# Three classical blocks and three pairs of whole blocks in pass 1, with attention packed into fewer steps

## Chip, cores and metric

The kernel runs on one core of one Trainium2 chip. The metric is the device time of one launch in microseconds. An execution taken with the profiler has a time of its own, which stands beside the median of the unprofiled runs.

## What is computed

The reference is a softmax linear attention followed by two mixture-of-experts layers with one expert each. All data are float32.

```python
q_s = softmax(q, axis=-1)             # q, k, v: (8, 8, 576, 64)
k_s = softmax(k, axis=2)              # over the 576 positions
kv  = einsum('bhsd,bhse->bhde', k_s, v)
x   = einsum('bhsd,bhde->bhse', q_s, kv)
x   = x reshaped to (4608, 512)       # tokens x model width
h   = x @ w_in;  g = h * sigmoid(1.702 h);  x = g @ w_out      # moe, w_in 512x2048
h   = x @ w_in;  g = where(h >= 1, h, where(h <= -1, 0, (h + 1)**2 / 4));  out = g @ w_out   # moe2
```

## The kernel before

Every factor of a large product is split into a high and a low part in the fast matmul type, and each product is three matmuls: high by high, high by low, low by high. A "step" of the classical form is 512 tokens (a block, of which there are nine) by 128 columns of w_in: four slices of the model width by three, so 12 matmuls of 512 columns (`gemm1`, L1038 to L1040, into `hps`). A step of the other form (`gemm_b`, L1360, into `z` and `zx`) is one of seven products of Strassen's scheme over a pair of halves: also 12 matmuls, of as many columns as a half has tokens. Seven such steps do the work of eight classical steps of that many columns; there are four groups of seven, `g`, in a pair.

The program has four passes, one for each weight. Pass 1 multiplies by the first w_in. Its first 64 steps are the classical blocks `CL`, 0, 1, 2 and 4. Between them, attention for all nine blocks is computed: SP loads k, v and q; VectorE takes maxima of k (`m`, `mx`), TensorE transposes them (`pa`, L884) and spreads them (`pb`), VectorE subtracts (`kt`, L900), ScalarE takes the exponentials, TensorE makes `pk` (k by v), VectorE divides it to `kv`; on the q side VectorE makes `qm`, `qt`, `qz` and the division `qt<-qt,qz`, TensorE transposes (`pt`, L981) and multiplies by `kv` (`px`, L999). ScalarE and VectorE write a classical block's result to `x_sb` (`x_hi`, `x_lo`); any other block goes through `xs` to DRAM. Meanwhile VectorE and ScalarE make Strassen's sums of the first weight (`t_pieces`, eight times eleven VectorE operations and three ScalarE copies, in `ts` and `w`). After the 64 steps come the pairs `PAIRS`, with halves of 384, 448 and 448 columns, which read `xs` back; in that stage w_out of the first layer is loaded raw and converted (`Weights("out1")`, conversion at L178 on ScalarE) and its products are stored for pass 2. Pass 2 starts at L1517; passes 3 and 4 are L605 and L487.

Nothing of pass 1's order is written by hand. `Plan` collects pieces: an engine, an estimated length `ns`, a rank in steps, names read and written, and for transfers `moves`, the time that the memory is busy. `order` simulates the engines by these estimates, takes at each moment the piece that can start first (the lowest rank among those that can start then), and so fixes each engine's order. `LATE` is the delay that it puts between a piece and its readers. Ranks are in units of a step of TensorE: attention of block j starts at `AT[j]`, and a new block starts every 6 steps.

Of the kernel before, what the change touches and what calls it, by code (L numbers as in the profile page):

```python
# [17 lines left out]
class Plan:  # L18
# [14 lines left out]
    def add(self, engine, ns, rank, fn, reads=(), writes=(), moves=0, take=0, give=0, haste=0, table=None):  # L33
        self.pieces.append(
            (rank, len(self.pieces), engine, ns, fn, reads, writes, moves, take, give, rank - haste, table)
        )

    def order(self):
        pieces = sorted(self.pieces, key=lambda x: x[:2])
        wrote, read, needs, after = {}, {}, [], [[] for _ in pieces]  # L40
        for n, (_, _, _, _, _, reads, writes, *_) in enumerate(pieces):
            deps = {wrote[r] for r in reads if r in wrote}
            for w in writes:
                deps |= {wrote[w]} if w in wrote else set()
                deps |= set(read.pop(w, ()))
                wrote[w] = n
            for r in reads:
                read.setdefault(r, []).append(n)
            deps.discard(n)
            needs.append(len(deps))  # L50
            for d in deps:
                after[d].append(n)
        since = [0] * len(pieces)
        free = dict.fromkeys(self.LATE, 0)
        open_to = {e: [n for n, x in enumerate(pieces) if x[2] == e and not needs[n]] for e in free}
        banks, moved, out, table = [0] * self.banks, 0, [], None

        def when(e, n):
            take = pieces[n][8]
            if take > len(banks):  # L60
                return None
            return max(free[e], since[n], sorted(banks)[take - 1] if take else 0)

        while len(out) < len(pieces):
            best = None
            for e, ns in open_to.items():
                starts = [(t, n) for n in ns if (t := when(e, n)) is not None]
                if starts:
                    first = min(t for t, _ in starts)
                    pick = min((pieces[n][10], n) for t, n in starts if t <= first)[1]  # L70
                    if best is None or first < best[0]:
                        best = first, e, pick
            start, e, n = best
            _, _, _, ns, _, _, _, moves, take, give, _, needed = pieces[n]
# [24 lines left out]
def kernel(  # L99
# [18 lines left out]
    CL = (0, 1, 2, 4)  # L118
# [4 lines left out]
    NB = NT // TB  # L123
# [88 lines left out]
    class Weights:  # L212
# [16 lines left out]
        def load(self, si, i, put):  # L229
# [14 lines left out]
            put(0, "SP", 560, fn, (), self.raw_n[i], moves=10.5 * n)  # L244
# [141 lines left out]
    O_AT = {"s7": 20, "u2": 21, "c11": 22, "c12": 23, "u3": 20, "c22": 23, "d11": 23}  # L386
# [201 lines left out]
    def pass_in(xq, sl, hooks):  # L588
# [140 lines left out]
        def later(k0, lag=1):  # L729
            def put(k, engine, ns, fn, reads, writes, moves=0):  # L730
                add(engine, ns, k0 + k, fn, reads + step(int(k0 + k) - lag), writes, moves, haste=H[5])
            return put
# [62 lines left out]
    AT = {0: (-20, -14), 1: (1, 5)}  # L795
    AT.update({j: (8.6 + 6.0 * (j - 2), 8.6 + 3.3 + 6.0 * (j - 2)) for j in range(2, NB)})
# [219 lines left out]
    def x_hi(j, c):  # L1016
        if c == 0:
            x0 = (20, 8)[j % 2]
# [34 lines left out]
    def keys(b, first, n, u):  # L1053
# [4 lines left out]
        def put(k, engine, ns, fn, reads, writes, **kw):  # L1058
            add(engine, ns, u + k, fn, reads, writes, **kw)
# [21 lines left out]
    def attention(j, at):  # L1081
        b = j if j < B else None
        x = CL.index(j) % 2 if j in CL else 0
        if b is not None:
            n = 1 if j == 0 else 2
            for first in range(0, 2, n):
                keys(j, first, n, at[first] + (4 if j else 0))
        for p in range(2):
# [5 lines left out]
            def put(k, engine, ns, fn, reads, writes, u=u, **kw):  # L1094
                add(engine, ns, u + k, fn, reads, writes, **kw)

            v0 = at[0] + (3.1 + 1.4 * p if j > 1 else 1.6 + 3 * p + V_AT) if j else u + V_AT
            if b is not None:
                k0 = (at[0] - 1 + 2 * p if j > 1 else at[0] - 6 + 4.3 * p) if j else u - 6
                put(k0 - u, "SP", 1120, lambda p=p: load_k(b, p), step(int(k0) - 1),  # L1100
                    tuple(nk[0] + (i,) for i in range(2)), moves=1800)
            put(-5, "SP", 1120 * (2 if j else 1), lambda t=t: load_q(t), step(int(u) - 6), nf, moves=1600)
            if b is not None:
                for h in range(5):
                    by = 0.25 if j > 1 else V_BY
                    put(v0 - u + h * by, "SP", 600, lambda p=p, h=h: load_v(b, p, h),
# [19 lines left out]
            at_px = 10 + (at[1] - u) * (j == NB - 1) + p / 10  # L1126
# [34 lines left out]
    add("PE", 0, AT[NB - 1][1] + 10.86, new_slots, px + old_t, sl(*BUSY))  # L1161
    add("PE", 0, AT[NB - 1][1] + 10.85, new_banks, px + old_t, (("bank", 2), ("bank", 3)))
# [51 lines left out]
    def t_pieces(u, m):  # L1214
        g, ns = m // 2, 90 + 1.06 * 256
        rows, k = (m, m + 1), [u]
# [5 lines left out]

        def part(x):
            return t_raw[x] if isinstance(x, int) else f32(t_at(x[0], *rows)[x[1]])

        def name(x):
            return (("ts", x),) if isinstance(x, int) else w_names(x[0], g)[x[1]:x[1] + 1]
# [4 lines left out]
        def high(p, x):  # L1232
            do("ACT", lambda: copy(t_at(p, *rows)[0], t_raw[x]), (("ts", x),) + free, w_names(p, g)[:1])

        def low(p, x):
            do("DVE", lambda: tt(t_at(p, *rows)[1], t_raw[x], part((p, 0)), ALU.subtract),
                (("ts", x),) + w_names(p, g)[:1] + free, w_names(p, g)[1:])
# [77 lines left out]
    PAIRS = ((384, 0), (448, 768), (448, 1664))  # L1315
# [3 lines left out]
    EB = ((24, 25, 26, 18, 19) * 7)[:32] + (E1 + E2) * 2  # L1319
# [113 lines left out]
    def later(k0, lag=1, haste=-3):  # L1433
        def put(k, engine, ns, fn, reads, writes, moves=0):
            add(engine, ns, k0 + k, fn, reads + step(int(k0 + k) - lag), writes, moves, haste=haste)
# [4 lines left out]
    hand(AT[NB - 1][1] + 10.88, sl(*WB), w_new.names)  # L1440
    NEXT = LAST + len(steps)
    w_new.everything([AT[NB - 1][1] + 11 + 5.3 * i for i in range(8)], lambda k: later(k, 1, 1))
# [260 lines left out]
```

## Time and profile before

| | us |
|---|---|
| median of 3 runs | 1516.66 |
| lowest and highest | 1516.39 to 1518.07 |
| the profiled execution | 1521.21 |
| its span | 1519.2 |
| startup, to the first L1038 | 31.65 |
| classical stage, to the first L1360 | 234.59 |
| pairs, to the first L1517 | 202.41 |
| passes 2 to 4, to the end of the span | 1050.55 |

The granted TensorE clock is 0.995 of full speed over the span, which is the level of 2.4 GHz. TensorE is busy for 98% of the span. A row of the trace that ends in brackets gives the idle time before the instruction and what released it.

### The profile page before, as it was taken

The page shows a single profiled execution, that of the slowest core. Times are in us where ns is not written, and L with a number is a line of the kernel's source. Part 1 is how long each engine was busy: PE and PEld are TensorE (multiplying, and loading weights), DVE is VectorE, ACT ScalarE, POOL GpSimd, SP SyncE. Part 2 cuts the span into 40 slices and gives each one's busy share as a digit, 9 for nine tenths or more (in the row PEclk, how much of TensorE's full clock was granted, in tenths as well). Part 3 has the DMA queues.
Part 4 walks back from the last instruction along what each step waited for, and adds up shares of the span by engine and source line. Part 5 has one row for each costly group of instructions (what it writes and reads, how often), then busy time and mean ns, then how long its engine had stood idle before and what let it go on. Part 6 is the DMA issues. An engine that isn't in the chain of part 4 may idle for free.

```text
span 1519.2 us, 21451 instructions
## 1 busy us (share of the span) xinstructions
PE 1483.9 (98%) x7920; PEld 1298.7 (85%) x7920; DVE 1132.6 (75%) x1470; ACT 904.3 (60%) x1154; POOL 6.2 (0%) x27
## 2 busy tenths in 40 slices
PE   5999999999999999999999999999999999999998
PEld 3777777998998888879998788888999788888998
DVE  7999993664627798899885486767675878686885
ACT  5878884575744454555545587878777444343442
POOL 0000000000000000000000000000000000000000
PEclk9999999999999999999999999999999999999999
DMA  9977755878798866676859555555668971625341
GB/s 282 280 228 214 216 191 188 282 246 284 236 329 323 325 215 235 208 243 208 273 171 392 198 202 226 196 219 193 248 232 323 380 245 53 201 86 151 93 126 42
DMA packets 276457, 341.17 MB, mean 225 GB/s; under 512 B 97152, under 2 KB 235904, under 8 KB 274560
## 3 DMA queue, kind: packets, MB, share of 16 engines
q1 hardware_dynamic: 275552, 339.70, 66.3%
q8 instruction: 62, 1.02, 0.3%
q14 instruction: 43, 0.35, 0.1%
q10 hardware_dynamic: 800, 0.10, 0.0%
HBM read 196.08 MB, written 143.65 MB: 224 GB/s over the span
## 4 chain that ended last, share of the span: by engine, by line
PE 85%; DMA 8%; DVE 3%; issue 1%; SPq 1%; ACT 1%; DVEq 0%; ACTq 0%
PE z L1517 16%; PE z L605 12%; PE z L487 12%; PE zx L605 9%; PE zx L487 9%; PE z L1360 5%; PE hps L1038 4%; PE zx L1360 4%; PE hps L1040 4%; PE hps L1039 4%; PE zx L1517 3%; DVE s L209 2%; DMA g<-s 2%; DMA w<-in_moe_w_in_dram 1%; DMA wp_in<-s 1%
## 5 line engine op out<-in xcount | busy, mean ns | idle before, releaser
L209 DVE TENSOR_TENSOR s<-s,s 128x1024 fp32r<-128x1024 f32 (+7 forms) x692 | 607.5, 920 | 146.2 <-PE zx L487 32.0
L1517 PE MATMUL z<-s,w 128*128 128x512 f32 (+1 forms) x1440 | 297.2, 367 | 1.2 <-DVE s L209 1.2
L1517 PEld LDWEIGHTS z<-s,w 128*128 128x128 f32 x1440 | 262.0, 188 | 35.5 <-DVE s L209 1.9
L455 ACT ACTIVATE s<-s 128x1024 fp32r<-128x1024 f32 (+1 forms) x140 | 136.3, 976 | 175.2 <-PE zx L487 62.1
L1190 ACT ACTIVATE s<-s 128x1024 fp32r<-128x1024 f32 (+2 forms) x168 | 161.5, 968 | 117.9 <-PE z L1517 67.4
L487 PE MATMUL z<-s,w 128*128 128x512 f32 (+1 forms) x1008 | 210.6, 368 | 1.3 <-DVE s L209 1.3
L605 PE MATMUL z<-s,w 128*128 128x512 f32 (+1 forms) x960 | 206.9, 367 | 0.0
L487 PEld LDWEIGHTS z<-s,w 128*128 128x128 f32 x1008 | 183.7, 188 | 26.1 <-DVE s L209 1.8
L605 PEld LDWEIGHTS z<-s,w 128*128 128x128 f32 x960 | 175.1, 188 | 22.6
L605 PE MATMUL zx<-s,w 128*128 128x512 f32 (+1 forms) x720 | 160.3, 371 | 5.1 <-ACT s L1190 4.6
L605 PEld LDWEIGHTS zx<-s,w 128*128 128x128 f32 x720 | 132.8, 190 | 23.2 <-ACT s L1190 5.0
L487 PE MATMUL zx<-s,w 128*128 128x512 f32 (+1 forms) x648 | 135.1, 367 | 0.0
L487 PEld LDWEIGHTS zx<-s,w 128*128 128x128 f32 x648 | 117.9, 188 | 15.0
L1360 PE MATMUL z<-s,w 128*128 128x448 f32 (+1 forms) x576 | 117.1, 355 | 0.0
L1360 PEld LDWEIGHTS z<-s,w 128*128 128x128 f32 x576 | 105.6, 188 | 6.0
L1038 PE MATMUL hps<-s,w 128*128 128x512 f32 x256 | 104.7, 409 | 0.9 <-ACT s L1044 0.9
L1040 PE MATMUL hps<-s,w 128*128 128x512 f32 x256 | 100.5, 392 | 0.0
L1039 PE MATMUL hps<-s,w 128*128 128x512 f32 x256 | 100.3, 392 | 0.0
L1360 PE MATMUL zx<-s,w 128*128 128x448 f32 (+1 forms) x432 | 89.5, 356 | 3.9 <-ACT zx L1190 3.6
L1360 PEld LDWEIGHTS zx<-s,w 128*128 128x128 f32 x432 | 79.1, 188 | 9.4 <-ACT zx L1190 4.3
L282 ACT ACTIVATE s<-s 128x256 fp32r<-128x256 f32 x168 | 65.1, 409 | 30.0 <-DVE s L209 13.6
L209 DVE TENSOR_TENSOR s<-s,z 128x1024 f32<-128x1024 f32 (+2 forms) x58 | 63.7, 1099 | 23.7 <-PE z L605 8.0
(102 smaller groups left out, 1477.2 us busy)
## 6 DMA issues: line engine op xcount, KB each, us to landing
s<-g SPq DMA_DIRECT2D x96, 512.0 KB, 5.7
g<-s SPq DMA_DIRECT2D x80, 512.0 KB, 2.9
wp_out<-s SPq DMA_DIRECT2D x112, 256.0 KB, 2.7
w<-wp_out SPq DMA_DIRECT2D x14, 2048.0 KB, 13.5
g<-s SPq DMA_DIRECT2D x48, 384.0 KB, 3.3
s<-g SPq DMA_DIRECT2D x48, 384.0 KB, 4.3
s<-in_moe_w_out_dram SPq DMA_DIRECT2D x32, 512.0 KB, 5.0
wp_in<-s SPq DMA_DIRECT2D x56, 256.0 KB, 4.2
```

The source lines that it names most:

```text
L209: return nc.vector.tensor_tensor(out=o, in0=x, in1=y, op=op)
L282: nc.scalar.activation(out=hi, in_=src, func=ACTF.Copy, scale=-1.0 if neg else 1.0)
L455: first_of[s] = nc.scalar.activation(out=hi, in_=src, func=ACTF.Copy)
L487: nc.tensor.matmul(out=z[:, m, :n], lhsT=a, rhs=b[:, c, :], start=(at is not None and i == 0 and c == 0 and x == 0), stop=(i == 3 and c == ...
L605: nc.tensor.matmul(out=z[:, m, :n], lhsT=a, rhs=b[:, c, :], start=(p in OPENS and c == 0 and x == 0), stop=(c == 1 and x == 2), skip_group ...
L1038: nc.tensor.matmul(out=hps, lhsT=wh, rhs=ah, start=(kk == 0), stop=False)
L1039: nc.tensor.matmul(out=hps, lhsT=wh, rhs=al, start=False, stop=False)
L1040: nc.tensor.matmul(out=hps, lhsT=wl, rhs=ah, start=False, stop=(kk == KD - 1))
L1190: nc.scalar.activation(out=o, in_=x, func=ACTF.Copy)
L1360: nc.tensor.matmul(out=zb[jj, g, a][:, m, :n], lhsT=w[:, f], rhs=y[:, c, :], start=(p in OPENS and c == 0 and x == 0), stop=(c == 1 and x ...
L1517: nc.tensor.matmul(out=zs2[j, a][:, m, :n], lhsT=y, rhs=b[:, c, :], start=(first and c == 0 and x == 0), stop=(i == 3 and c == 1 and x == ...
```

## The change

Block 4 is no longer a classical block. There are 48 classical steps, for blocks 0, 1 and 2, and three pairs with halves of 512 columns, which are six whole blocks. Attention of a block now starts every 4 steps (`PACE`), with the ranks inside a block scaled by 4/6, so it ends at step 42.7 by its ranks and not at 58.8. The sums of the first weight start at steps 30, 40, 46 and 52 (20, 29, 38 and 47 before); the last two groups use a tile of another slot, `late`, and their ranks lie behind the classical stage. The first w_out's raw loads and conversions start at 42.8 and come every 5 steps. A raw weight load counts 2,500 ns more until its readers may start in the planner's simulation (`lands`). Several slots are dealt out anew. Passes 2 to 4 issue the same TensorE instructions in the same order.

```diff
-    CL = (0, 1, 2, 4)
+    CL = (0, 1, 2)
...
-            put(0, "SP", 560, fn, (), self.raw_n[i], moves=10.5 * n)
+            put(0, "SP", 560, fn, (), self.raw_n[i], moves=10.5 * n, lands=2500)
...
-            late = done + self.LATE[e]
+            late = done + self.LATE[e] + lands
...
-    AT = {0: (-20, -14), 1: (1, 5)}
-    AT.update({j: (8.6 + 6.0 * (j - 2), 8.6 + 3.3 + 6.0 * (j - 2)) for j in range(2, NB)})
+    PACE = 4.0
+    AT = {0: (-20, -14), 1: (0, 3)}
+    AT.update({j: (9 + PACE * (j - 2), 9 + 0.55 * PACE + PACE * (j - 2)) for j in range(2, NB)})
+    END = AT[NB - 1][1] + PACE / 0.6 + 0.85
...
-            add(engine, ns, u + k, fn, reads, writes, **kw)
+            add(engine, ns, u + k * f, fn, reads, writes, **kw)
...
+        f = PACE / 6 if j > 1 else 1
...
-    add("PE", 0, AT[NB - 1][1] + 10.86, new_slots, px + old_t, sl(*BUSY))
+    add("PE", 0, END, new_slots, px + old_t, sl(*BUSY))
...
-        rows, k = (m, m + 1), [u]
+        rows, k, ts = (m, m + 1), [u], ("ts", "tu")[g >= T_LATE]
...
+        def raw(x):
+            if ts == "ts":
+                return t_raw[x]
+            if "late" not in t_ops:
+                t_ops["late"] = slot(T_SLOT).rearrange("p a c -> p (a c)")
+            return t_ops["late"][:, 256 * x:256 * x + 256].rearrange("p (a f) -> p a f", a=1)
...
+    T_AT_STEP, T_LATE, T_SLOT = (30, 40, 46, 52), 2, 19
+    late = ("tu", 0), ("tu", 1)
+    hand(END + 0.03, sl(T_SLOT), late)
+    hand(T_AT_STEP[-1] + 1.9, late, sl(T_SLOT))
...
-            t_pieces((20, 29, 38, 47)[g] + m, 2 * g + m)
+            t_pieces(T_AT_STEP[g] + m, 2 * g + m)
...
-    PAIRS = ((384, 0), (448, 768), (448, 1664))
+    PAIRS = ((512, 0), (512, 1024), (512, 2048))
...
-    EB = ((24, 25, 26, 18, 19) * 7)[:32] + (E1 + E2) * 2
+    EB = ((24, 25, 26, 18) + (24, 25, 26, 18, 19) * 6)[:32] + (E1 + E2) * 2
...
-    w_new.everything([AT[NB - 1][1] + 11 + 5.3 * i for i in range(8)], lambda k: later(k, 1, 1))
+    w_new.everything([END + 0.14 + 5 * i for i in range(8)], lambda k: later(k, 1, 1))
...
-    hand(LAST - 15, even, sl(*QB.values()))
-    hand(LAST - 0.05, odd, sl(*CB[4], *CB[3]))
+    hand(LAST - 15, odd, sl(*QB.values()))
+    hand(LAST - 0.05, even, sl(*CB[4], *CB[3]))
...
-                operand_b(0, x, AT[NB - 1][1] + 10.9 + 0.9 * i if i < 5 else LAST + i - 3.8)
+                operand_b(0, x, END + 0.04 + 0.9 * i if i < 5 else LAST + i - 3.8)
```

VectorE, from the division that makes `kv` to the division of the queries, in the classical stage. `ts` and `w<-ts` are the sums of the first weight, `qz` and `qt` the queries, `mc<-pa` the keys' maxima of the next block. Before:

```order
L209 TENSOR_TENSOR kv_318<-pk,rs 128x256
L209 TENSOR_TENSOR w<-ts_326,w 128x256
L209 TENSOR_TENSOR w<-ts_327,w 128x256
L209 TENSOR_TENSOR ts_326<-w 128x256
L209 TENSOR_TENSOR ts_327<-w 128x256
L209 TENSOR_TENSOR qt<-qf,qm 128x4x4x64
L209 TENSOR_TENSOR ts_326<-ts_326,ts_327 128x256
L968 TENSOR_REDUCE qz<-qt 128x16
L209 TENSOR_TENSOR w<-ts_326,w 128x256
L972 TENSOR_SCALAR qz<-qz 128x16
L973 RECIPROCAL qz<-qz 128x16
L209 TENSOR_TENSOR qt<-qt,qz 128x1024
```

and now:

```order
L209 TENSOR_TENSOR kv_319<-pk,rs 128x256
L209 TENSOR_TENSOR qt<-qf,qm 128x4x4x64
L974 TENSOR_SCALAR qz<-qz 128x16
L975 RECIPROCAL qz<-qz 128x16
L209 TENSOR_TENSOR qt<-qt,qz 128x1024
L890 TENSOR_REDUCE mc<-pa 128x4
L944 TENSOR_REDUCE qm<-qf 128x16
L970 TENSOR_REDUCE qz<-qt 128x16
L209 TENSOR_TENSOR ts_328<-ts_328,ts_329 128x256
L974 TENSOR_SCALAR qz<-qz 128x16
L975 RECIPROCAL qz<-qz 128x16
```

Of the first kind six rows in twelve belonged to the weight's sums, of the second one in eleven; the queries of one half and the keys of the next block follow each other directly.

TensorE, around a transpose `pa` of the keys' maxima. Before, it stands alone between two steps:

```order
L1039 MATMUL hps<-s_971,w 128x512
L1040 MATMUL hps<-s_969,w 128x512
L1038 MATMUL hps<-s_969,w 128x512
L1039 MATMUL hps<-s_971,w 128x512
L1040 MATMUL hps<-s_969,w 128x512
L884 MATMUL pa<-ident,mx 128x128 x4
L1038 MATMUL hps<-s_1266,w 128x512
L1039 MATMUL hps<-s_1268,w 128x512
```

and now:

```order
L1042 MATMUL hps<-s_946,w 128x512
L918 MATMUL pk<-v_317,kt 64x65 x20
L918 MATMUL pk<-v_318,kt 64x65 x20
L983 MATMUL pt<-ident,qt 128x128 x8
L886 MATMUL pa<-ident,mx 128x128 x4
L1040 MATMUL hps<-s_945,w 128x512
L1041 MATMUL hps<-s_947,w 128x512
```

Now `pk` of both halves, the transposes of the queries (`pt`) and `pa` of the next block stand together with no step between them, so `pt` and `pa` have no large matmuls ahead of them that could cover a late VectorE.

ScalarE, in the stage of the pairs, around the conversion of a raw weight (L178, two halves) and the copy `zx<-z` that a step of TensorE needs. Before:

```order
L1395 ACTIVATE s_3072<-s_3072 128x2x384
L1190 ACTIVATE w<-even 128x256
L178 ACTIVATE s_2888<-s_2887 128x512
L1395 ACTIVATE s_3076<-s_3076 128x2x384
L1395 ACTIVATE s_3156<-zx 128x2x384
L178 ACTIVATE s_2888<-s_2890 128x512
L1190 ACTIVATE zx<-z 128x2x384
L1190 ACTIVATE w<-even 128x256
```

and now:

```order
L1409 ACTIVATE s_3272<-z 128x1024
L1193 ACTIVATE s_3274<-s_2803 128x1024
L1193 ACTIVATE s_3291<-s_2780 128x1024
L178 ACTIVATE s_2632<-s_2631 128x512
L1409 ACTIVATE s_3230<-s_3230 128x1024
L178 ACTIVATE s_2632<-s_2634 128x512
L1409 ACTIVATE s_3252<-s_3252 128x1024
L1193 ACTIVATE zx<-z 128x1024
```

The copy of the bank still stands behind both halves of the conversion, with one row between the second half and it, where before there was none.

## Rows read from the trace of the kernel before

**Rows 1.** The page: span, and TensorE's busy time, share and instructions

```profile
span 1519.2 us, 21451 instructions
PE 1483.9 (98%) x7920; PEld 1298.7 (85%) x7920; DVE 1132.6 (75%) x1470; ACT 904.3 (60%) x1154; POOL 6.2 (0%) x27
```

**Rows 2.** Waits of TensorE: line, releaser, us in total, times, longest

```profile
PE zx L1360 <- ACT zx L1190: 3.6, 2, 2.0
...
PE hps L1038 <- ACT s L1044: 0.9, 1, 0.9
```

**Rows 3.** Timeline of TensorE at three stage borders: start, length, line, shapes

```profile
31.65 0.78 PE L1038 MATMUL hps<-s,w 128*128 128x512 f32 x1
...
266.24 2.27 PE L1360 MATMUL z<-s,w 128*128 128x384 f32 x12
268.35 0.39 PE L1038 MATMUL hps<-s,w 128*128 128x512 f32 x1
...
468.65 1.54 PE L1517 MATMUL z<-s,w 128*128 128x512 f32 x6
```

**Rows 4.** The chain of waits: unbroken runs of matmuls, start, length, count

```profile
366.66 4.86 PE z L1360 x24
...
501.46 65.28 PE z L1517 x288
...
1052.07 4.18 PE z L605 x24
```

**Rows 5.** Windows: stretch, length, five engines' busy time, PEclk, DMA share, GB/s

```profile
37.00:227.10 190.10, 189.18 (x1530) 150.41 (x1529) 180.55 (x295) 159.44 (x186) 3.08 (x10) 1.00 0.79 226
60.00:80.00 20.00, 20.00 (x183) 15.22 (x182) 19.54 (x29) 18.86 (x21) 0.61 (x2) 1.00 1.04 269
180.00:200.00 20.00, 20.00 (x178) 16.12 (x176) 17.43 (x34) 15.42 (x20) 0.00 (x0) 1.00 0.84 257
266.20:468.60 202.40, 198.51 (x1021) 186.57 (x1021) 107.04 (x189) 118.72 (x178) 0.00 (x0) 1.00 0.81 280
```

**Rows 6.** VectorE's groups, 37 to 240 us: count, busy, mean ns, idle before

```profile
L900 DVE TENSOR_TENSOR kt<-kt,pb 128x1280 f32<-128x1280 f32 x14 | 20.5, 1483 | 0.5 <-PE pb L893 0.5
L209 DVE TENSOR_TENSOR qt<-qt,qz 128x1024 f32<-128x1024 f32 x16 | 19.6, 1225 | 0.6
...
L209 DVE TENSOR_TENSOR ts<-w 128x256 f32<-128x256 f32 x32 | 12.8, 419 | 0.1
...
L209 DVE TENSOR_TENSOR s<-px,s 128x512 fp32r<-128x512 f32 x14 | 9.2, 684 | 1.9 <-ACT s L1020 1.9
```

**Rows 7.** Timeline of VectorE, the last division of the queries in the classical stage

```profile
224.69 0.75 DVE L209 TENSOR_TENSOR ts<-w 128x256 f32<-128x256 f32 x2
225.36 0.17 DVE L972 TENSOR_SCALAR qz<-qz 128x16 f32<-128x16 f32 x1
...
225.85 1.23 DVE L209 TENSOR_TENSOR qt<-qt,qz 128x1024 f32<-128x1024 f32 x1
```

**Rows 8.** DMA issues, 30 to 240 us: count, KB each, median us to landing

```profile
g<-s SPq DMA_DIRECT2D x26, 512.0 KB, 4.3
v<-in_v_dram SPq DMA_DIRECT2D x55, 128.0 KB, 3.9
kt<-in_k_dram SPq DMA_DIRECT2D x12, 512.0 KB, 5.7
...
xs<-qT SPq DMA_DIRECT2D x8, 512.0 KB, 4.3
```

**Rows 9.** Who waited for the loads of k (line 848): us, times

```profile
  DVE m L209: 8.6, 5
```

**Rows 10.** Timeline of ScalarE and TensorE where a pair's step waited

```profile
285.04 0.69 ACT L178 ACTIVATE s<-s 128x512 f32<-128x512 f32 x1 [3.19 <-DMA s<-in_moe_w_out_dram]
...
288.48 0.68 ACT L178 ACTIVATE s<-s 128x512 f32<-128x512 f32 x1 [1.32 <-DMA s<-in_moe_w_out_dram]
...
289.91 2.35 PE L1360 MATMUL zx<-s,w 128*128 128x384 f32 x12 [1.97 <-ACT zx L1190]
```

More of the change, by code (lines that the diff above doesn't have):

```diff
@@ L31, in __init__, with add @@
         self.pieces, self.banks, self.chained = [], banks, chained
-    def add(self, engine, ns, rank, fn, reads=(), writes=(), moves=0, take=0, give=0, haste=0, table=None):
+    def add(self, engine, ns, rank, fn, reads=(), writes=(), moves=0, take=0, give=0, haste=0, table=None, lands=0):
         self.pieces.append(
-            (rank, len(self.pieces), engine, ns, fn, reads, writes, moves, take, give, rank - haste, table)
+            (rank, len(self.pieces), engine, ns, fn, reads, writes, moves, take, give, rank - haste, table, lands)
         )
@@ L73, in order @@
             start, e, n = best
-            _, _, _, ns, _, _, _, moves, take, give, _, needed = pieces[n]
+            _, _, _, ns, _, _, _, moves, take, give, _, needed, lands = pieces[n]
             ns += self.SWAP * (needed not in (None, table))
@@ L384, in bank @@
         return rooms["p", i].tile([P, 2, TB], FP32, tag=f"p{i}", name=name)
-    O_AT = {"s7": 20, "u2": 21, "c11": 22, "c12": 23, "u3": 20, "c22": 23, "d11": 23}
+    O_AT = {"s7": 20, "u2": 21, "u3": 23, "c22": 20, "d11": 20}
     T_AT = (22, 23)
@@ L729, in later, with put @@
         def later(k0, lag=1):
-            def put(k, engine, ns, fn, reads, writes, moves=0):
+            def put(k, engine, ns, fn, reads, writes, moves=0, lands=0):
                 add(engine, ns, k0 + k, fn, reads + step(int(k0 + k) - lag), writes, moves, haste=H[5])
@@ L1017, in x_hi @@
         if c == 0:
-            x0 = (20, 8)[j % 2]
+            x0 = (8, 20)[j % 2]
             x_sb[j] = [[slot(x0 + 2 * i + c, FP32R) for c in range(2)] for i in range(2)]
@@ L1051, in step, with keys @@
         return (("step", s),) if s >= 0 else ()
-    def keys(b, first, n, u):
+    def keys(b, first, n, u, f):
         ps = range(first, first + n)
@@ L1086, in attention @@
             for first in range(0, 2, n):
-                keys(j, first, n, at[first] + (4 if j else 0))
+                keys(j, first, n, at[first] + (4 * f if j else 0), f)
         for p in range(2):
@@ L1125, in attention @@
             need += tuple(("kv", bb, p) for bb in range(2))
[L1126 removed]
+            at_px = 10 + (at[1] - u) / f * (j == NB - 1) + p / 10
             put(at_px, "PE", 1000, lambda p=p: q4(j, p), need, (("px", p),), take=2)
@@ L1221, in do @@
             add(engine, ns, k[0], fn, reads, writes)
+        def raw(x):
[4 more added lines that the diff above has]
+            return t_ops["late"][:, 256 * x:256 * x + 256].rearrange("p (a f) -> p a f", a=1)
         def part(x):
-            return t_raw[x] if isinstance(x, int) else f32(t_at(x[0], *rows)[x[1]])
+            return raw(x) if isinstance(x, int) else f32(t_at(x[0], *rows)[x[1]])
         def name(x):
-            return (("ts", x),) if isinstance(x, int) else w_names(x[0], g)[x[1]:x[1] + 1]
+            return ((ts, x),) if isinstance(x, int) else w_names(x[0], g)[x[1]:x[1] + 1]
         def dve(o, x, y, op):
@@ L1232, in high @@
         def high(p, x):
-            do("ACT", lambda: copy(t_at(p, *rows)[0], t_raw[x]), (("ts", x),) + free, w_names(p, g)[:1])
+            do("ACT", lambda: copy(t_at(p, *rows)[0], raw(x)), ((ts, x),) + free, w_names(p, g)[:1])
         def low(p, x):
-            do("DVE", lambda: tt(t_at(p, *rows)[1], t_raw[x], part((p, 0)), ALU.subtract),
-                (("ts", x),) + w_names(p, g)[:1] + free, w_names(p, g)[1:])
+            do("DVE", lambda: tt(t_at(p, *rows)[1], raw(x), part((p, 0)), ALU.subtract),
+                ((ts, x),) + w_names(p, g)[:1] + free, w_names(p, g)[1:])
         def both(x, y, op):
@@ L1433, in later, with put @@
     def later(k0, lag=1, haste=-3):
-        def put(k, engine, ns, fn, reads, writes, moves=0):
-            add(engine, ns, k0 + k, fn, reads + step(int(k0 + k) - lag), writes, moves, haste=haste)
+        def put(k, engine, ns, fn, reads, writes, moves=0, lands=0):
+            add(engine, ns, k0 + k, fn, reads + step(int(k0 + k) - lag), writes, moves, haste=haste, lands=lands)
         return put
```

18 lines of the change are left out of this document (9 added, 9 removed).

## Prediction, made before the change was run

> **What bounds the kernel now.** I read the page first: TensorE is busy for 1483.9 us of a span of 1519.2, 98% [rows 1], so time can be saved only by giving TensorE less to do or by taking away the little idle time it has. Then its waits: in pass 1 it lost 3.6 us to a ScalarE copy in the pair stage and 0.9 us at `hps` [rows 2]. Then the borders of the stages: classical from 31.65, pairs from 266.24, pass 2 from 468.65, with one last classical step inside the pair stage, from 268.35 on [rows 3]. Last, the windows, for who is close behind TensorE: in the classical stage VectorE, busy for 180.55 of 190.10 us, with ScalarE at 159.44; in the pair stage nobody (VectorE 107.04, ScalarE 118.72 of 202.40) [rows 5]. So the change must be judged by two things: how many matmul columns go, and whether VectorE still keeps up when attention is packed more tightly.
>
> **Matmul columns.** Unbroken runs give the pace: 65.28 us for 288 matmuls of 512 columns, 226.7 ns each; 4.86 for 24 of 448, 202.5 ns; 4.18 for 24 of 384, 174.2 ns [rows 4]. Each step is 12 matmuls, each pair 28 steps, 336 matmuls. Before: 64 classical steps, 768 x 0.2267 = 174.1; pairs 336 x 0.1742 + 672 x 0.2025 = 194.6; 368.7 us. After: 48 classical steps, 576 matmuls, and 3 x 336 = 1008, all of 512 columns: 1584 x 0.2267 = 359.1. That is **-9.6**. All of it lies on the bottleneck, and nothing else runs on TensorE in its place: attention's small matmuls are the same in number.
>
> The Trainium skill ("TensorE: Matmul & The Clock Gate", section "Back-to-back issue gap") gives a fixed 2.5 ns on top of N/2.4 ns; this trace disagrees, with 226.7 where that makes 215.8. By the page the sum here would be -5.7 (an estimate), since wide matmuls would be worth less against narrow ones; the measured runs decide.
>
> **The pair stage.** It took 468.65 - 266.24 = 202.4 us, without the classical step (12 x 0.2267 = 2.7) 199.7, against 194.6 of pure matmul time. The excess is 5.1 us, and 3.9 of it can be named: 3.6 where `zx` waited for ScalarE [rows 2] and small change. The timeline shows how: ScalarE stood 3.19 us and then 1.32 us in front of a conversion whose raw weight had not landed, and the copy that TensorE's next step needed was queued behind it; TensorE lost 1.97 us [rows 10]. After, the planner puts 2.5 us between such a load and its conversion, so conversions should stand later in ScalarE's queue. But the copy still stands behind both halves of a conversion in the listing of after, so the mechanism isn't gone by construction; the real landing time decides. Steps are longer (2.72 us, not 2.1 to 2.4), which gives ScalarE more room for each. Bounds: 0 if no load is late, 5 if it goes as before. I take 2, nearer to the loads being in time, since only two of eight conversions cost TensorE anything before. Stage: **-5.1 + 2 = -3.1**. In this stage VectorE also gets the second half of the first weight's sums, some 44 operations of 0.34 to 0.42 us, 15 to 18 us; it had 95 us free there [rows 5], so that costs nothing as long as the sums come before the steps that read them, which the listing has some steps ahead.
>
> **The classical stage.** Its matmuls are counted above; what remains are waits. The stage before had 0.9 us of them at `hps` [rows 2], put there by a late result of attention; I count **-0.9** and then the new waits on their own. A new block came every 6 steps and now every 4. Per block TensorE has 4 x 2.72 = 10.9 us of steps and about 7.8 of attention: 234.6 us of stage less 63 x 2.72 = 171.4 is 63.2, over some eight blocks. So 18.7 us a block, where it was 24.1.
>
> VectorE has to fit in. I take the stretch from its second `kv` division to the last division of the queries, 37.0 to 227.1 in the trace: 190.1 us, VectorE busy for 180.55 of them [rows 5, 7]. In the listings the same stretch has 10 steps fewer on TensorE: 190.1 - 27.2 = 162.9 us. On VectorE it has 57 sums of the weight fewer (29 where there were 86) and 4 of the low-part subtractions `s<-px,s` fewer. A sum costs 12.8/32 = 0.40 by its group's busy time [rows 6], or 0.335 where two follow each other (224.69 to 225.36) [rows 7]; the subtraction 9.2/14 = 0.66 [rows 6]. So VectorE sheds 22 to 25.5 us and keeps 155 to 159 of work for 162.9 of TensorE's. If it never waits, it is in time on the average, and only its worst place is late. But before, it also stood idle for 9.6 us of the stretch, mostly behind others: 8.6 us in all for loads of k [rows 9], 1.9 for ScalarE [rows 6]. If it waits as much again, it needs 165 to 169 and TensorE loses 2 to 6. The listings say where: TensorE's `pt` waits for the division of the queries and `pa` for the maxima of k, and they now follow `pk` with no step between them, so a late VectorE is no longer covered by 2.72 us of matmuls. Behind a waiting `pt` everything on TensorE stands still, since its queue runs in order. ScalarE was busy for 159.44 of the stretch [rows 5]; if it shed nothing it would still fit into 162.9, and it sheds the copies that go with the 57 sums, so I count it at nothing.
>
> Memory is the other load. A block moves k and v, 1.18 MB each by their shapes, q and `xs` 1.05 each, and two stores of `g`, 0.52 each: 5.5 MB in 18.7 us, 294 GB/s, where the stretch has 226 now [rows 5, 8]. The nearest rows: at 60 to 80 us the engines were full (share 1.04) at 269 GB/s, so a block would take 5.5/0.259 = 21.3 us; at 180 to 200 they were at 0.84 with 257, so full would be 306 GB/s, 18.0 us [rows 5]. The two stand on either side of 18.7. I take new waits of **+6**: the upper end of VectorE's sum, with k's loads later than they were. Bounds: 0 (no waits) and 18.2 (memory at its slower rate, below).
>
> The Trainium skill ("DMA: Bandwidth & Descriptors", section "Specifications") gives about 358 GB/s as a core's share of the memory: 5.5 MB would take 15.4 us (an estimate) and not bind. It also asks for pieces of 512 bytes or more for full rate; the loads of v come in rows of 64 floats, 256 bytes, and the trace's 269 GB/s at full share bears that second rule out. It speaks against this change, and is the last rival below.
>
> **The rest.** Passes 2 to 4 have the same TensorE instructions in the same order. What may differ is how pass 2 is entered (its first operands and the conversions of the next weight); **-0.5**, with -1.5 to +2.
>
> **Sum.** -9.6 - 5.1 + 2 - 0.9 + 6 - 0.5 = -8.1. The profiled execution stands at 1521.21, so after it would be near 1513.1; the median 1516.66 is 4.55 lower than that execution, and the same difference on it gives **1508.6**.
>
> **Rivals.** (1) *Waits nearly vanish.* VectorE keeps 155 to 159 us of work for 162.9 and uses the difference; no new waits, pair stage at +1.5: -9.6 - 5.1 + 1.5 - 0.9 - 0.5 = -14.6, 1502.1. Against it: TensorE lost 0.9 us even at 24.1 us a block, and the cover between attention's groups is gone. (2) *The gain is eaten.* VectorE falls behind by its own waits at each of seven blocks, about 1.7 us each, W = 12 in place of 6: -2.1, 1514.6, no difference that can be told. For it: loads of k made VectorE wait 8.6 us already, and they are now asked for at a higher rate. Against it: VectorE has 4 to 8 us to spare over the stretch. (3) *Slower: memory becomes the bound of the blocks.* At the slower rate each of seven blocks takes 21.3 us and not 18.7, 18.2 in place of 6: +4.1, 1520.8. It decides from 14.1 us of waits on, that is 20.7 us a block. For it: share 1.04 at 60 to 80 us. Against it: at 180 to 200 nearly the same rate took a share of only 0.84. That the change doesn't do what it says (conversions as late as before) is worth 3 us and lies inside the range.
>
> **Chances.** Forecast 0.66, rival (1) 0.12, (2) 0.14, (3) 0.08. A measurement of this kernel tells apart about 0.2%, 3.0 us: faster is below 1513.6, slower above 1519.7. Forecast and (1) are faster, 0.78; (2) 0.14 the same; (3) 0.08 slower. The range: the forecast with its bounds (pair waits 0 to 5, classical waits 0 to 12, pass 2 -1.5 to +2, which will hardly all fall on one side), 1502.5 to 1515.0; it leaves out half of (1), some of (2) and all of (3), about 0.2.
>
> **What will show it.** In the trace of after: the first `gemm_b` near 31.65 + 234.6 - 15 x 2.72 + 5 = 230; the pair stage near 231 (228.5 of matmuls and 2 of waits); then passes 2 to 4 of the same length, 1050. Waits of TensorE at `pt`, `pa` or `hps` for VectorE of about 6 us; if they stand for DMA of k or v, (3) has begun. DMA share near 1 and VectorE with idle time in the blocks' windows would say memory; VectorE at 98 to 99% with TensorE waiting would say VectorE. Waits of `zx` for ScalarE should be below 3.6. The prediction is wrong if classical waits pass 11 us, or if the pair stage takes more than 234.

## The result, and the profile after

| | before | after |
|---|---|---|
| median of the runs, us | 1516.93 | 1502.25 |
| lowest and highest | 1516.39 to 1518.07 | 1501.48 to 1506.35 |
| the profiled execution / its span | 1521.21 / 1519.2 | 1501.64 / 1499.6 |
| startup, to the first step of gemm1 | 31.65 | 30.96 |
| classical stage | 234.59 | 195.16 |
| pairs | 202.41 | 228.48 |
| passes 2 to 4, to the end of the span | 1050.55 | 1045.0 |

The ratio of after to before is 0.9906, with a 95% interval from 0.9893 to 0.992: 14 us faster, between 12 and 16. Forecast were 1508.6, in a range from 1502.5 to 1515.0; the first rival, in which the waits nearly vanish, stood at 1502.1. So the median lies at the lower end of the range, a quarter of a microsecond outside it.

The span fell by 19.6 us and the median by 14.7. The execution that was profiled before stood 4.5 us above its median, so the stages of these two traces add up to more than the medians differ. One part of it recurs, though: pass 3 took 353.08 us before and 349.22 after, and in the other traces below it is likewise shorter wherever the change is in. What is behind that stands in the section on the prediction.

The page of after, its span and its busy row, as [rows 1]:

```profile
span 1499.6 us, 21008 instructions
...
PE 1470.7 (98%) x7728; PEld 1266.3 (84%) x7728; DVE 1140.2 (76%) x1466; ACT 899.2 (60%) x1138; POOL 6.2 (0%) x27
```

The timeline of TensorE at the borders of the stages, as [rows 3]. gemm1 now has the lines 1040 to 1042, a pair's step 1374, pass 2 1531:

```profile
30.96 0.76 PE L1040 MATMUL hps<-s,w 128*128 128x512 f32 x1
...
226.12 3.11 PE L1374 MATMUL z<-s,w 128*128 128x512 f32 x13
...
454.60 1.75 PE L1531 MATMUL z<-s,w 128*128 128x512 f32 x7
```

The pair stage is 454.60 - 226.12 = 228.48 us. Its 1008 matmuls at 226.7 ns are 228.5: not a gap is left in it. The chain of waits shows the pace, as [rows 4]:

```profile
226.28 5.44 PE z L1374 x24
231.72 2.72 PE zx L1374 x12
```

TensorE's waits after its start-up, over the whole span, as [rows 2]. No row of L1374 is left, and `hps` waits 1.4 us where it waited 0.9 (the rows of `pa` and `pb` mix in the start-up; what they wait in the classical stage stands below):

```profile
PE zx L605 <- ACT zx L675: 2.3, 1, 2.3
PE hps L1040 <- ACT s L1046: 1.4, 2, 0.8
PE z L487 <- DVE s L209: 1.2, 1, 1.2
```

Two windows of after, as [rows 5]: the stretch of blocks, and the pairs (columns: stretch, length, busy time of PE, PEld, DVE, ACT and POOL, granted clock, DMA share, GB/s).

```profile
37.00:200.00 163.00, 160.25 (x1404) 126.23 (x1403) 156.06 (x228) 133.39 (x152) 3.08 (x10) 1.00 0.89 261
...
226.20:454.60 228.40, 228.40 (x1010) 189.11 (x1008) 133.06 (x234) 138.05 (x193) 0.00 (x0) 1.00 0.74 270
```

The first window was given the length that the prediction worked out, 163 us, and in it VectorE has the work that was counted, 156.06 us (155 to 159), and 6.9 us of idle time where the prediction carried over 9.6. The stretch itself begins earlier than the prediction has it: the second division of `kv` starts at 31.75 in before, not at 37.0, and at 30.49 in after. From there to the end of the last division of the queries, before and after:

```profile
31.75:227.08 195.33, 194.41 (x1553) 153.81 (x1552) 185.59 (x302) 161.51 (x191) 3.08 (x10) 1.00 0.79 230
```

```profile
30.49:201.81 171.32, 168.57 (x1442) 132.28 (x1441) 164.03 (x241) 140.00 (x162) 3.08 (x10) 1.00 0.89 263
```

It became 24.0 us shorter, where 27.2 were counted. VectorE's idle time in it fell from 9.7 to 7.3 us, and TensorE's rose from 0.9 to 2.8.

### The profile page after: what moved, and what is told of

Same layout as the page of the kernel before. It is cut to its first block, busy times and chain, and to the rows that moved or that the text cites. A ratio compares the mean times of both kernels' runs of the same rounds, so it can differ in the third digit from the quotient of the medians.

```text
span 1499.6 us, 21008 instructions
## 1 busy us (share of the span) xinstructions
PE 1470.7 (98%) x7728; PEld 1266.3 (84%) x7728; DVE 1140.2 (76%) x1466; ACT 899.2 (60%) x1138; POOL 6.2 (0%) x27
## 4 chain that ended last, share of the span: by engine, by line
PE 89%; DMA 6%; DVE 3%; SPq 1%; issue 1%; ACT 1%; DVEq 0%; ACTq 0%
PE z L1531 20%; PE z L487 12%; PE z L605 12%; PE zx L605 9%; PE zx L487 9%; PE z L1374 9%; PE zx L1374 7%; PE zx L1531 3%; PE hps L1040 2%; PE hps L1042 2%; PE hps L1041 2%; DMA kt<-in_k_dram 1%; DMA qf<-in_q_dram 1%; DMA g<-s 1%; DMA s<-x 1%; PE px L1001 1%
## 5 line engine op out<-in xcount | busy, mean ns | idle before, releaser
L209 DVE TENSOR_TENSOR s<-s,s 128x1024 fp32r<-128x1024 f32 (+5 forms) x692 | 614.3, 927 | 157.7 <-ACT s L282 33.6
L1531 PE MATMUL z<-s,w 128*128 128x512 f32 (+1 forms) x1440 | 296.7, 367 | 0.0
L1531 PEld LDWEIGHTS z<-s,w 128*128 128x128 f32 x1440 | 262.1, 188 | 33.8
L455 ACT ACTIVATE s<-s 128x1024 fp32r<-128x1024 f32 (+1 forms) x140 | 136.2, 976 | 176.1 <-PE zx L487 62.1
L1193 ACT ACTIVATE s<-s 128x1024 fp32r<-128x1024 f32 (+1 forms) x168 | 164.9, 988 | 125.5 <-PE z L1531 87.6
L1374 PE MATMUL z<-s,w 128*128 128x512 f32 x576 | 136.4, 389 | 0.0
L1374 PEld LDWEIGHTS z<-s,w 128*128 128x128 f32 x576 | 108.1, 188 | 22.5
L1374 PE MATMUL zx<-s,w 128*128 128x512 f32 x432 | 103.8, 389 | 0.0
L1374 PEld LDWEIGHTS zx<-s,w 128*128 128x128 f32 x432 | 81.1, 188 | 16.8
L209 DVE TENSOR_TENSOR s<-s,z 128x1024 f32<-128x1024 f32 (+1 forms) x58 | 65.9, 1135 | 24.3 <-PE z L605 8.0
L1040 PE MATMUL hps<-s,w 128*128 128x512 f32 x192 | 79.0, 411 | 1.4 <-ACT s L1046 1.4
L655 ACT ACTIVATE s<-s 128x1024 f32<-128x1024 f32 (+1 forms) x80 | 77.3, 969 | 1.1
L282 ACT ACTIVATE s<-s 128x256 fp32r<-128x256 f32 x168 | 63.9, 408 | 22.8 <-DMA wp_in<-s 10.7
L1042 PE MATMUL hps<-s,w 128*128 128x512 f32 x192 | 75.1, 391 | 0.0
```

What stands on the lines that cost most here:

```text
L209: return nc.vector.tensor_tensor(out=o, in0=x, in1=y, op=op)
L282: nc.scalar.activation(out=hi, in_=src, func=ACTF.Copy, scale=-1.0 if neg else 1.0)
L455: first_of[s] = nc.scalar.activation(out=hi, in_=src, func=ACTF.Copy)
L655: nc.scalar.activation(out=got["t"], in_=got["t"], func=ACTF.Square)
L1040: nc.tensor.matmul(out=hps, lhsT=wh, rhs=ah, start=(kk == 0), stop=False)
L1042: nc.tensor.matmul(out=hps, lhsT=wl, rhs=ah, start=False, stop=(kk == KD - 1))
```

## The experiments

All are edits of the changed kernel, but for two that edit the kernel before. Each ratio is to the kernel before, run beside it. The changed kernel itself was run again as a base:

> The changed kernel unaltered, as the base for the runs beside it: 1502 us, between 1500 and 1504. Both theories expect the same.

It gave 0.9899 (0.9873 to 0.9924), a median of 1504.77 beside 1519.78 for before, and in its trace a classical stage of 195.8 us and pairs of 228.5. Medians moved by up to 3 us from one set of runs to another, so small differences are read by ratio and by stage.

### The landing allowance, taken out and put in alone

```diff
-            put(0, "SP", 560, fn, (), self.raw_n[i], moves=10.5 * n, lands=2500)
+            put(0, "SP", 560, fn, (), self.raw_n[i], moves=10.5 * n, lands=0)
```

> The changed kernel with the 2500 ns for the landing of raw weight loads taken out of the planner (lands=0). Theory A (the pair stage lost its 5 us of excess because conversions now stand later than their loads land): waits of zx for ScalarE behind conversions are back, 2 to 5 us, 1504 to 1507. Theory B (the longer steps, 2.72 us instead of 2.1 and 2.4, gave ScalarE the room, and the landing allowance did nothing): within 1 us of the changed kernel, no waits of zx.

The second edit gives the kernel before `lands` in `Plan` and 2500 in this call, and nothing else.

> The kernel before with the landing allowance alone (2500 ns, raw weight loads). Theory A: the waits of 3.6 us at zx for ScalarE go, 1512 to 1514.5. Theory B (longer steps did it): the waits stay, 1515.5 to 1518.

Without it the changed kernel has a ratio of 0.9925 (0.9901 to 0.9948), 3 us behind the base by its median and 4 by its ratio, though the intervals overlap; its pair stage is 231.3 us where the base has 228.5, and pass 2 takes 346.2 instead of 345.0. With it alone, the kernel before has 0.9978 (0.9966 to 0.999), 3.3 us faster. ScalarE's waits in the pair stage tell why. First of the kernel before, then of the changed kernel without the allowance, then of before with it (the changed kernel has no such row at all):

```profile
ACT s L178 <- DMA s<-in_moe_w_out_dram: 13.0, 9, 4.2
```

```profile
ACT s L178 <- DMA s<-in_moe_w_out_dram: 10.7, 8, 2.5
```

```profile
ACT s L178 <- DMA s<-in_moe_w_out_dram: 0.2, 1, 0.2
```

ScalarE stood for 13.0 us before conversions whose raw weight hadn't landed, and the planner, told of 2.5 us more, puts other work of ScalarE there. Theory A holds in both directions. Its size by the traces is 2.8 us of the pair stage in the changed kernel (231.3 against 228.5), but only 1.6 in the kernel before (200.8 against 202.4), though TensorE's waits at `zx` fell there by 3.3 us, from 3.9 to 0.6. The difference lies in the matmuls: in the trace of before with the allowance all those of 448 columns took 206.7 ns where they took 202.5 without it, 2.8 us over 672 of them. They are the same in number and shape, and why they took longer stays open.

```profile
PE zx L1360 <- DVE s L209: 0.6, 1, 0.6
```

```profile
343.91 4.96 PE z L1360 x24
```

With the allowance pass 2 is shorter too, by 1.3 us in the one kernel and 1.7 in the other (346.7 to 345.0); that this is the allowance's isn't shown, since the next run, which lacks it, has 345.1 as well. Theory B has a part too: without the allowance the longer steps still let ScalarE wait for 10.7 us, but TensorE then loses only 1.5 us at `zx`, where it lost 3.9:

```profile
PE zx L1374 <- DVE s L209: 0.8, 2, 0.5
PE zx L1374 <- ACT s L1193: 0.7, 2, 0.4
```

### The price of a column

```diff
-    PAIRS = ((384, 0), (448, 768), (448, 1664))
+    PAIRS = ((512, 0), (512, 1024), (256, 2048))
```

in the kernel before, with its four classical blocks.

> The kernel before with the pairs cut into halves of 512, 512 and 256 columns instead of 384, 448 and 448: the same products over the same 2560 tokens. Theory A (a matmul costs by its columns, and 512 is the cheapest width per column): 672 x 0.2267 + 336 x 0.1134 = 190.4 against 194.6, 4 us faster than before. Theory B (a fixed cost weighs on the narrow ones, 0.130 us by the step from 448 to 512): 195.9, 1 us slower; the 256-column steps of 1.4 to 1.6 us may also be too short for ScalarE and VectorE, and add waits.

The ratio is 0.9987 (0.9976 to 0.9998), 2 us faster, between the two. The chain of waits has the price that was missing:

```profile
421.45 2.87 PE z L1360 x24
```

A matmul of 256 columns takes 119.6 ns, so the stage's matmuls come to 672 x 0.2267 + 336 x 0.1196 = 192.5, 2.1 less than 194.6 (the stage itself took 199.6 us where it took 202.4). Of the change's 9.6 us this kind of saving is a part: five blocks in halves of 512 would take 2.5 x 336 x 0.2267 = 190.4, 4.2 less than before; the other 5.4 come from block 4, whose 16 steps of 2.72 us become half a pair, 14 steps.

### How much more VectorE could carry

Half of the sums of the first weight stay out of the stretch of attention. This puts most of them back:

```diff
-    T_AT_STEP, T_LATE, T_SLOT = (30, 40, 46, 52), 2, 19
+    T_AT_STEP, T_LATE, T_SLOT = (20, 26, 32, 38), 4, 19
```

> The changed kernel with all sums of the first weight in the old tile and at ranks 20, 26, 32 and 38, so that 66 of the 88 stand ahead of the last division of the queries where the change has 29. Theory A (VectorE is what the classical stage has to fit, and the later sums make it fit): VectorE had 156.06 us of work in the 163.0 us from 37 to 200; 37 sums more at 0.335 to 0.40 make it 168 to 171, so TensorE loses 5 to 8 us there, up to 15 if VectorE keeps its 6.9 us of idle time; in all 1507 to 1517, with waits at hps, pa or pt for VectorE. Theory B (VectorE's load didn't matter; other things, memory or the order, set the stage): within 1 us of the changed kernel.

It gave 0.9893 (0.9871 to 0.9916), no different from the base. The classical stage is 196.2 us (195.8 in the base), with VectorE busy for 187.83 in 31 to 227 where the changed kernel has 181.65 in 31 to 226:

```profile
31.00:227.00 196.00, 192.62 (x1570) 150.93 (x1568) 187.83 (x314) 154.82 (x195) 3.08 (x10) 0.99 0.83 249
```

Theory A fell as it was put. VectorE's last division of the queries ends at 212.6 us instead of 201.8, so the sums did make attention later; but the planner, which knows their length, had put more classical steps ahead of it, and steps were left to put there (the stage ends at 227). It isn't without a mark: TensorE waited once for 2.6 us at `hps`, and the granted clock then stood at 1.2 GHz for 3.4 us; even so the stage is longer by 1 us at most. Only when VectorE gets slower behind the planner's back does it cost. That is the next pair of runs, in which the order is that of the changed kernel:

```diff
         nc.vector.tensor_reduce(out=mx, in_=st["qf", t], axis=AX.X, op=ALU.max)
+        if t % 2 == 0:
+            nc.vector.tensor_reduce(out=mx, in_=st["qf", t], axis=AX.X, op=ALU.max)
```

> The changed kernel, its order unchanged, with the maxima of the queries (1.21 us) computed twice for every other pair of heads: about 8 reductions, 9 to 10 us more on VectorE in the classical stage, where it is busy for 181.8 of 195.1 us in the changed kernel. Theory A (VectorE's idle 13 us are a reserve: TensorE has steps enough to cover it): 0 to 3 us slower than the changed kernel. Theory B (VectorE is the pace of the stage, its idle time lies at fixed waits): 9 us slower.

and without the condition:

> The same for all pairs of heads: 15 to 17 reductions, 18 to 20 us more on VectorE. Theory A: the reserve of 13 us is used up, 5 to 8 us slower than the changed kernel. Theory B: 18 us slower. A third case, memory as the bound with VectorE hidden behind it: no difference.

In the trace the first adds 7 reductions, 8.5 us, to the stretch of attention, the second 15, 18.3 us. The classical stage takes 199.5 and 208.5 us, 4 and 13 more than 195.2 to 195.8; the ratios are 0.9919 (0.9899 to 0.9938) and 0.9983 (0.9971 to 0.9995). So some 4.5 us are covered, and beyond it VectorE's time is TensorE's, almost one for one (9.8 us more of VectorE, 9.0 of TensorE, of which some 1.6 are the clock's: it stood at 1.2 GHz for 3.4 us from 101.1 on, around waits of 1.0 and 2.2 us at `pa`). It lies between the theories: there is a reserve, but of a third of VectorE's idle 13 us; the rest of the idle time covers nothing. TensorE's waits in the classical stage, of the changed kernel and of the second run:

```profile
PE hps L1040 <- ACT s L1046: 1.4, 2, 0.8
PE pa L886 <- DVE mx L209: 0.9, 1, 0.9
PE pb L895 <- DVE mc L890: 0.4, 2, 0.2
```

```profile
PE pa L886 <- DVE mx L209: 8.6, 5, 2.3
PE hps L1041 <- ACT s L1047: 3.0, 2, 2.1
PE pb L895 <- DVE mc L890: 0.6, 3, 0.2
```

The place is `pa`, the transpose that now has no steps ahead of it. In the other direction:

```diff
-        nc.vector.tensor_reduce(out=mx, in_=st["qf", t], axis=AX.X, op=ALU.max)
+        nc.vector.tensor_reduce(out=mx, in_=st["qf", t][..., :16], axis=AX.X, op=ALU.max)
```

> The changed kernel, order unchanged, with the maxima of the queries taken over the first 16 of 64 numbers only: each of 15 to 17 reductions costs about 0.3 us instead of 1.21, some 14 us less on VectorE in the classical stage. Theory A (the 2.75 us for which TensorE still waits in that stage are VectorE's): 1 to 2.75 us faster than the changed kernel. Theory B (VectorE waits for loads and copies there, which stay where they are): within 1 us.

The maxima cover 16 of 64 numbers. A reduction took 0.41 us instead of 1.21, 12 us less over fifteen, and in the window VectorE was busy for 10.8 us less (145.30 where it had 156.06):

```profile
37.00:200.00 163.00, 159.67 (x1404) 126.04 (x1403) 145.30 (x228) 133.17 (x151) 3.08 (x10) 1.00 0.87 261
```

The ratio is 0.9891 (0.9873 to 0.9908), the classical stage 195.4 us: nothing gained. VectorE's idle time grew by what was taken away (17.7 us where it was 6.9). At the order of the changed kernel VectorE's work is therefore not what is left to save; the prediction's sum for VectorE had it as the pace.

### Memory

```diff
...
-        nc.sync.dma_start(out=g0_dram[CL[j]][m // 2], in_=st.pop(("sg", s)))
+        sg = st.pop(("sg", s))
+        nc.sync.dma_start(out=g0_dram[CL[j]][m // 2], in_=sg)
+        nc.sync.dma_start(out=g0_copy[j][m // 2], in_=sg)
```

> The changed kernel with every store of g in the classical stage sent to a second place in DRAM as well: 24 stores of 0.52 MB, 12.6 MB more in the 195 us, where 255 GB/s at a DMA share of 0.84 flow in the changed kernel; 319 GB/s are asked for. If memory is close to binding (the last rival, 259 to 306 GB/s at full share): 8 to 40 us slower. If it has headroom, or only late loads of k count: under 3 us slower.

The ratio is 0.9949 (0.9932 to 0.9966), and the classical stage took 205.3 us, 9.5 more than the base. The stretch of blocks, as the window above:

```profile
37.00:200.00 163.00, 153.58 (x1275) 120.75 (x1274) 146.34 (x210) 126.07 (x142) 3.07 (x10) 0.98 1.00 302
```

The engines of DMA are full (share 1.00) at 302 GB/s. It fits the length: 255 GB/s over 195.1 us are 49.8 MB, with the 12.6 added 62.4, and at 302 GB/s these take 206.6 us. TensorE then waits for v itself, and VectorE for k 11.0 us where it waited 2.4. Around the longest wait for v, 3.2 us, the granted clock stood at 1.2 GHz for 6.8 us, so a part of the 9.5 us may be the clock's:

```profile
PE pk L919 <- DMA v<-in_v_dram: 4.6, 2, 3.2
PE pa L887 <- DVE mx L210: 2.5, 2, 1.5
```

So memory is close behind. A block's 5.5 MB take 18.2 us at this rate, half a microsecond less than the 18.7 us at which the blocks are spaced.

What the engines move at full share depends on the size of the packets. In the trace of after, 37 to 200 us, packets of 256 bytes took 19.3 ns, of 1024 bytes 57.1 and of 4096 bytes 169.8: 213, 287 and 386 GB/s on 16 engines. A fifth of the bytes came in packets of 256, v above all, and took 28% of the engines' time:

```profile
DMA packets 55654, 42.59 MB, mean 261 GB/s; under 512 B 36176, under 2 KB 50000, under 8 KB 55637
```

The stores that were doubled are in packets of 4096 bytes, so at full share the run with them moves more than the changed kernel would (261 GB/s at a share of 0.89 is 293).

### The pace of the blocks

```diff
-    PACE = 4.0
+    PACE = 3.6
```

> The changed kernel with blocks every 3.6 steps: 17.6 us a block, less than memory's 18.2 at 302 GB/s and about VectorE's 17 to 18. Theory A (a block is then bound by memory or VectorE): 7 blocks x 0.6 to 1 us, 3 to 7 us slower. Theory B (the planner spaces the blocks by its own estimates and the rank hardly matters): within 1 us.

The ratio is 0.9898 (0.9884 to 0.9912), the classical stage 196.5 us: theory B. VectorE's last division of the queries ended at 204.0 us, no earlier than at pace 4 (201.8). It fits that the planner's own costs space the blocks, as soon as the ranks ask for more than it thinks the engines can do.

```diff
-    PACE = 4.0
+    PACE = 4.5
...
-    T_AT_STEP, T_LATE, T_SLOT = (30, 40, 46, 52), 2, 19
+    T_AT_STEP, T_LATE, T_SLOT = (30, 40, 47.5, 53), 2, 19
```

> The changed kernel with attention's blocks every 4.5 steps instead of 4 (END 46.8, the sums of the third group moved to step 47.5 behind it). A block then has 20 us instead of 18.7 for VectorE's 17 to 18 and for memory's 18.2 (5.5 MB at 302 GB/s). Theory A (the blocks' pace is what TensorE still waits for): 1 to 2.5 us faster. Theory B (the reserve suffices at 4, and a later end of attention only delays the first operands of the pairs): 0 to 4 us slower, with waits at the first steps of the pairs.

By these ranks the operands of the first pair's last two products (49.2 and 50.2) come ahead of the fifth's (50.5), the likely reason that some values of this kernel are wrong; the work is of the same amount. The ratio is 0.9955 (0.9942 to 0.9968). The classical stage is 195.5 us, as at pace 4; the pair stage is 236.4, 8 longer, with waits at its steps:

```profile
PE z L1374 <- DVE s L209: 2.6, 2, 2.4
...
PE zx L1374 <- DVE s L209: 1.5, 1, 1.5
PE z L1374 <- ACT s L1193: 1.2, 1, 1.2
PE z L1374 <- ACT s L1409: 1.1, 1, 1.1
```

Theory A fell: more room for a block gains nothing in the classical stage. That the loss in the pairs comes from the late end of attention alone isn't shown, since the order of the operands changed with it.

```diff
-                k0 = (at[0] + (2 * p - 1) * f if j > 1 else at[0] - 6 + 4.3 * p) if j else u - 6
+                k0 = (at[0] + (2 * p - 2.5) * f if j > 1 else at[0] - 6 + 4.3 * p) if j else u - 6
```

> The changed kernel with each block's loads of k ranked one step (1.5 x 4/6) earlier. VectorE waited 2.4 us for k in the classical stage of the changed kernel. Theory A (late loads of k are what makes VectorE and so TensorE late): 1 to 2 us faster. Theory B (the load waits for its tile or for memory, not for its rank): within 1 us.

The ratio is 0.9881 (0.9866 to 0.9896), the fastest of all, with a classical stage of 193.9 us, 1.2 to 1.9 less than in the two traces of the changed kernel. VectorE's wait for k in the stretch fell from 2.4 to 1.0 us, that for q rose from 1.1 to 3.1. The intervals overlap, so it isn't shown to be faster than the changed kernel; if it is, it is by 1 to 4 us.

## Why the prediction was right, and where its sizes were off

Faster was right, and so was the mechanism by which it is mostly faster: fewer columns on TensorE, and no excess in the pairs. The sizes were not: the gain is nearly twice the 8.1 us that were forecast. By the stages of the two traces the largest misses are pass 3 (3.9 us), the classical stage (3.7) and the pairs (2).

| term, us | predicted | measured, from the stages of the two traces |
|---|---|---|
| matmul columns | -9.6 | -9.6: 228.48 for the pairs, all at 226.7 ns; 448 columns at the 202.5 ns of the trace of before |
| pair stage's excess | -5.1 + 2 | -5.1: no gap is left |
| classical stage, waits old and new | -0.9 + 6 | +1.4: 195.16 against 234.59 - 15 x 2.72 = 193.8 |
| entry to pass 2 and pass 2 | -0.5 | -1.7: 344.98 from the first L1531 to pass 3, 346.68 before |
| pass 3 | 0 | -3.9: 349.22, 353.08 before |
| startup | 0 | -0.7 |
| sum | -8.1 | -19.6 between the spans, with -14.7 between the medians |

A part of what separates the last two is the trace of before. The two other traces whose classical blocks are those of before (the allowance alone, and 512, 512 and 256) have 233.2 us for the classical stage, not 234.6, and 345.0 and 345.1 for pass 2, not 346.7. Against them the term of the classical stage would be some +2.8, that of pass 2 about nothing, and the sum some -16.5.

**The columns** held, at the price of 448 columns in that one trace; at the 206.7 ns of the run with the allowance alone the saving would be 12.4. The formula of the Trainium skill ("TensorE: Matmul & The Clock Gate", section "Back-to-back issue gap"), which is there the gap of a matmul by itself and by which the gain would have been 5.6 (the prediction has 5.7), doesn't agree with the trace of after either: 2.72 us for 12 matmuls are 226.7 ns, where it makes 215.8.

**The pair stage** was under-rated by 2 us. The step that was too careful is "the mechanism isn't gone by construction": ScalarE's queue still has the copy of the bank behind the conversion, but no conversion waits for its load any more. The two runs on the landing allowance show that it does most of it (2.8 us of the stage, or 3.3 of 3.9 us of waits); the rest probably goes with the longer steps.

**The classical stage** is the term that was mis-sized, +6 where TensorE's named waits in the stage come to 2.7 us, against the 0.9 of before. The failing sentence is "if it waits as much again": VectorE's idle time of 9.6 us was carried over as if it were work, but in 163 us it was 6.9, and TensorE's order covers some 4.5 us of lateness even with the groups of attention side by side. Its main reason was a row misread. The 8.6 us for loads of k in [rows 9] are those of the whole run, and 6.4 of them lie in the start-up; in the stretch VectorE waited 2.1 us for k before and 2.4 after, so the reason given for the second rival shrinks with it. Before, up to 31 us; before, 37 to 235; after, 37 to 205:

```profile
DVE m L209 <- DMA kt<-in_k_dram: 6.4, 3, 5.2
```

```profile
DVE m L209 <- DMA kt<-in_k_dram: 2.1, 2, 1.8
```

```profile
DVE m L209 <- DMA kt<-in_k_dram: 2.4, 2, 1.9
```

The mechanism was right, and a little more load brings it out: with 18 us more on VectorE it is `pa`, named in the prediction, at which TensorE waits 8.6 us. With the sum's lower end (VectorE has 4 to 8 us to spare) taken at its word, the first rival would have been the forecast. That it came within 0.2 us of the median is in part luck: it counted no new waits (2.7 us came), 1.5 us of waits for the pairs (none came) and nothing for pass 3.

**What was expected of the later sums** is not what they do. The prediction took the 57 sums that leave the stretch as what lets VectorE fit. Putting 37 of them back cost nothing that can be told from zero. So the later sums give room, which this program hardly needs.

**The slower rival**, memory as the bound of the blocks, did not come, but was near: its rate was between 259 and 306 GB/s, and the run with the doubled stores puts it at 302, 18.2 us a block and not 21.3. The window at 60 to 80 us, with its 269 GB/s at full share, was no measure of the whole stage. The Trainium skill's share of 358 GB/s for a core ("DMA: Bandwidth & Descriptors", section "Specifications") was not reached in this stage, but it isn't a bound either: around the start of pass 2 the trace of before has 388 GB/s.

```profile
460.00:480.00 20.00, 20.00 (x95) 17.40 (x94) 15.95 (x15) 10.07 (x12) 0.00 (x0) 1.00 1.04 388
```

The prediction saw the cost of 256-byte rows borne out by 269 GB/s at full share. That rate alone doesn't show it; the packets do, with 213 GB/s for 256 bytes against 386 for 4096. Whether the stage would be faster with wider rows of v wasn't tried.

**Pass 3** was put at nothing, as TensorE's instructions and their order there are the same. ScalarE's order is not. One copy of an operand stands in pass 3 behind four other activations in the kernel before, and ahead of pass 3 in the changed kernel. Before, TensorE waits 4.59 us for it:

```profile
835.35 1.04 ACT L1190 ACTIVATE s<-s 128x1024 fp32r<-128x1024 f32 x1
...
836.45 0.80 PE L605 MATMUL zx<-s,w 128*128 128x512 f32 x1 [4.59 <-ACT s L1190]
```

In that wait the granted clock fell to 1.2 GHz, and it stayed there for 6.8 us. After, the longest wait is the 2.3 us at `zx` shown above, and the clock stood low for 3.4 us. Two windows, before and after:

```profile
835.40:842.30 6.90, 5.39 (x12) 3.93 (x13) 2.02 (x2) 0.99 (x2) 0.00 (x0) 0.51 0.48 149
```

```profile
826.90:830.30 3.40, 3.40 (x10) 2.62 (x9) 1.23 (x1) 1.46 (x2) 0.00 (x0) 0.50 0.47 192
```

The waits (4.6 and 0.5 against 2.3 us) account for 2.8 of the 3.9 us, the clock for some 1.2. It isn't the chance of one execution: the kernel before and its two variants all have the wait of 4.6 us and 353.1 to 353.6 us for pass 3, the changed kernel and all its variants 2.2 to 3.2 us of wait and 347.6 to 350.3 us. Which part of the change moves the copy stays open; the allowance alone and the cut into 512, 512 and 256 alone don't.

## What to carry to other kernels

Count the columns that leave the bottleneck engine first; here they gave some 9.6 us, the largest part of the gain, and the price of every width came from unbroken runs of matmuls in the trace. When a wait is carried over from one kernel to the next, ask for it in the window that it is meant for: most of the 8.6 us for k lay in the start-up. Don't put a later stage at nothing because the bottleneck's instructions are the same there: another engine's order changed, and pass 3 gave 3.9 us. A planner that puts a conversion right behind its load needs the landing time in its estimate: 2.5 us of it, in one line, gave some 3 us in either kernel (in the changed one within the noise), because a ScalarE that waits holds back the copy queued behind it. And an engine's idle time is neither reserve nor need until it is loaded: adding 8.5 and 18.3 us to VectorE and taking 11 away told more than its 96% of busy time (156.06 of 163 us).

## What the runs showed of the hardware

At full share the DMA engines moved 302 GB/s in the mix of loads and doubled stores, and before 269 in one window of 20 us and 388 in another; packets of 256 bytes went at 213 GB/s and packets of 4096 at 386. TensorE's clock fell to 1.2 GHz in or just after waits of 4.6 us (pass 3 before) and 3.2 us (for v, with doubled stores), for 6.8 us each, and of 2.3 us (pass 3 after), for 3.4 us. It didn't fall at the same place in pass 3 in four of the runs, among them the one on 18 us more for VectorE, with a wait of 3.2 us. A matmul of 256 columns takes 119.6 ns, of 384 174.2, of 448 202.5 in one trace and 206.7 in another, of 512 226.7 (all at a granted clock of 1.00, the level of 2.4 GHz): a column gets dearer as the matmul gets narrower, 0.467 ns against 0.443, but by so little that cutting 2560 tokens into 512, 512 and 256 still gains 2 us over 384, 448 and 448.
